# Constants in another order, with padding: other start addresses for w_out_r, the x buffers and the work tiles

## The chip, the cores and the metric

The kernel runs on one core of a Trainium2 chip. The metric is the device time of one execution in microseconds. The core's engines are TensorE (PE; its weight loads are listed as PEld), VectorE (DVE), ScalarE (ACT), GpSimd (POOL) and SyncE (SP, which here only issues DMAs). The on-chip memory has 128 partitions; a tile [P, ...] takes the same bytes in each of them, and where it begins in a partition is its address in what follows.

## The reference

The input x has 8 batches of 3008 tokens with 256 features. Each batch goes through a Fourier layer along the tokens, and the result through a feed-forward layer. Cut to what is computed:

```python
X = np.fft.rfft(x, axis=1)                       # over 3008 tokens
Yr = X.real @ w_r - X.imag @ w_i + b_r
Yi = X.real @ w_i + X.imag @ w_r + b_i
Yr, Yi = soft(Yr), soft(Yi)                      # sign(v) * max(|v| - 0.01, 0)
y = np.fft.irfft(Yr + 1j * Yi, n=3008, axis=1).reshape(24064, 256)
h = y @ w_in                                     # 256 -> 2048
g = np.where(h > 0, h, np.exp(np.minimum(h, 0)) - 1)
out = g @ w_out                                  # 2048 -> 256
```

## The kernel before

The Fourier transforms are done as matrix products in two stages each (3008 = 47 x 64), with twiddle matrices M1 to M4 that the kernel computes at the start. The work of a batch is cut into units: A (first stage, reads x), X (second stage), M (the product with w_r and w_i, and the soft threshold), B and Y (the two stages back). Between A and X and between B and Y the data go through DRAM to change partitions.

The feed-forward layer is the main loop (lines 1050 to 1102). It has 376 steps: 47 blocks of 512 tokens, and in each 8 pairs of 128 hidden features. A step has three parts on TensorE:

- the front (`front_mm`, line 841): four matmuls, two for each of the pair's halves, that multiply w_in_s (bf16, the weights that are loaded) with 512 columns of yT (bf16, the operand that streams). Where a block lies over a batch's end, a matmul is split in two.
- a unit of the Fourier layer of a later batch, put between the front's halves. The planner (`units`, line 945) decides which, by due times and by what is ready. Not every step has one.
- the back (`back`, line 893) of the pair two steps earlier: eight matmuls that load 128 columns of gT (float32r, the activated hidden features) as weights, and stream one row block of w_out_r (float32r, 256 columns, that is 1 KB a partition).

Between front and back of a pair the activation is spread over ScalarE (exp, lines 855 to 858), GpSimd or VectorE (limit, lines 863 and 865) and VectorE (the sum, line 875, which writes gT).

Unit A (line 163) streams x from the buffers xt0 to xt2 in float32r, 512 columns a matmul, with M1 as weights. The other units stream bf16: unit M (line 262) wcat_r, wsum with 256 columns, unit B (line 356) Yt, unit X (line 197) M2, unit Y (line 397) M4.

In time, an opening of about 56 us builds the matrices, brings batch 0 through the Fourier layer and loads the weights (x and w_out_r through GpSimd's DMA queue, line 119 and line 701; all else through SyncE's). Then the main loop runs to the end.

Tiles get their addresses in the order in which they are made. The pool of constants comes first, and each tile takes its size rounded up to 32 bytes, so that a tile moves all that come behind it. The pools of work tiles follow in the order zp, wk1, wk2, wk3, wk4, xtp; then comes the staging pool of the opening, and in its place, after the opening, the pools gatep (the small tile that line 706 writes once), late2 (yT, osb), late3 (Et) and late1 (gT). The lines that set the addresses are 53 to 71 (constants), 425 (x buffers) and 705 (the gate tile):

```python
t = gatep.tile([P, 1], F32, name="gate", tag="gate")
nc.gpsimd.tensor_copy(t[0 : src.shape[0], :], src)
```

Of the kernel before, what the change touches and what calls it, by code (L numbers as in the profile page):

```python
# [8 lines left out]
ALU = mybir.AluOpType  # L9
AF = mybir.ActivationFunctionType  # L10
BF16 = mybir.dt.bfloat16
F32 = mybir.dt.float32
# [3 lines left out]
N1 = 47  # L16
N2 = 64
K1 = 24
# [7 lines left out]
def kernel(  # L26
# [11 lines left out]
    nc = tc.nc  # L38
    P = nc.NUM_PARTITIONS

    B, S, D = x.shape
# [10 lines left out]
    constp = ctx.enter_context(tc.tile_pool(name="constp", bufs=1))  # L52
    M1 = constp.tile([P, P], F32R, name="M1")
    M2 = constp.tile([2 * NR, NS, 2, 2 * K1], BF16, name="M2")
    M3 = constp.tile([P, K1, P], BF16, name="M3")
    M4 = constp.tile([4 * K1, 2 * N1], BF16, name="M4")
    wcat_r = constp.tile([P, 2, 2 * D], BF16, name="wcat_r")
    wsum = constp.tile([P, 2, 2, D], BF16, name="wsum")
    w_in_s = constp.tile([P, 2, DFF], BF16, name="w_in_s")
    w_out_r = constp.tile([P, NFT, E], F32R, name="w_out_r")  # L60
    bias_bc = constp.tile([P, 2 * D], F32, name="bias_bc")
    bias_d = constp.tile([P, D], F32, name="bias_d")
# [2 lines left out]
    dume = constp.tile([P, 1], F32, name="dume")  # L65
    w40 = constp.tile([P, 1], F32, name="w40")
    w41 = constp.tile([P, 1], F32, name="w41")
    arow_t = constp.tile([P, N1], F32, name="arow")
    v4 = constp.tile([P, N1], F32, name="v4")
    r4 = constp.tile([P, N1], F32, name="r4")  # L70
    sg3 = constp.tile([P, K1 // 2], BF16, name="sg3")

    dram = ctx.enter_context(tc.tile_pool(name="dram", bufs=2, space=bass.MemoryType.DRAM))
    zp = ctx.enter_context(tc.tile_pool(name="zp", bufs=1))
# [314 lines left out]
    def unit_Y(b, u, alone=False, on_dve=False):  # L389
# [6 lines left out]
        for j in range(8):  # L396
            nc.tensor.matmul(  # L397
                psv[:, j, 0 : 2 * N1], lhsT=Bs[:, j, dt * P : dt * P + P], rhs=M4[:],
                start=True, stop=True,
# [27 lines left out]
    with tc.tile_pool(name="stagep", bufs=1) as stagep:  # L427
# [19 lines left out]
        dve, pool = nc.vector, nc.gpsimd  # L447

        def iota(name, shape, pattern, base=0, cm=0, dt=F32, out=None):
            t = out if out is not None else stagep.tile(shape, dt, name=name)[:]  # L450
            nc.gpsimd.iota(
                t, pattern=pattern, base=base, channel_multiplier=cm,
                allow_small_or_imprecise_dtypes=True,
            )
            return t

        def row(name, shape):
            return stagep.tile(shape, F32, name=name)
# [45 lines left out]
        arow = iota("arow", [P, N1], [[1, N1]], out=arow_t[:])  # L504
# [37 lines left out]
        def points(g):  # L542

            gs, z = slice(8 * g, 8 * g + 8), slice(0, RZ)
            m_, k_ = mi[z, gs], kv[z, gs]
            dve.tensor_scalar(m_, m_, 63, None, ALU.bitwise_and)
            dve.scalar_tensor_tensor(
                k_, m_, float(N1), kk1[z].unsqueeze(1).to_broadcast([RZ, 8, K1, 2]),
                ALU.mult, ALU.add,
            )  # L550
            if g == 0:
                dve.scalar_tensor_tensor(
                    kv[z, 0, :, 1], mi[z, 0, :, 1], float(N1), kk1[z, :, 0], ALU.mult, ALU.add
                )
            kf = k_.rearrange("p s k t -> p s (k t)")
            dve.tensor_scalar(st[z, gs], kf, S // 2 + 0.5, -0.5, ALU.is_gt, ALU.add)
# [90 lines left out]
        dve.tensor_scalar(m3i[:], m3i[:], 63, None, ALU.bitwise_and)  # L647
        k3 = row("k3", [P, NV])
        dve.scalar_tensor_tensor(k3[:], m3i[:], float(N1), k1t[:], ALU.mult, ALU.add)
        dve.tensor_scalar(sg3[:], k3[:], S // 2 + 0.5, -0.5, ALU.is_gt, ALU.add)  # L650
        points(3)
        phases(3)
        wraps(2)
# [23 lines left out]
    gatep = ctx.enter_context(tc.tile_pool(name="gatep", bufs=2))  # L677
# [24 lines left out]

    def gate(src):

        t = gatep.tile([P, 1], F32, name="gate", tag="gate")
        nc.gpsimd.tensor_copy(t[0 : src.shape[0], :], src)


    def turn_M3(c):
# [6 lines left out]
    def fB(v, on_dve=False):  # L716
        unit_B(0, v, alone=True, on_dve=on_dve)

    load_w_in(0)
    gate(Z_of[0][:, 8, 0:1])  # L720
    for ci in range(3):
        load_x(1, ci)
# [19 lines left out]
    for o, src, sc, bi in ((1, w3, TURN, 0.0), (0, a3, -TURN, hpi[:])):  # L742
        nc.scalar.activation(
            M3f[0][:, :, o * N2 : o * N2 + N2], src[:], AF.Sin, bias=bi, scale=sc
        )
    sgb = sg3[:].unsqueeze(2).to_broadcast([P, K1 // 2, N2])
    nc.vector.scalar_tensor_tensor(
        M3f[1][:, :, 0:N2], M3f[0][:, :, N2:P], 2.0, sgb, ALU.mult, ALU.mult
    )
# [26 lines left out]
    fB(5, True)  # L776
    M4v = M4[:].rearrange("p (a h) -> p a h", h=2)
    for h, w in enumerate((w40, w41)):
# [354 lines left out]
```

## Time and profile before

| what | value |
|---|---|
| median of 3 runs | 884.86 us (883.47 to 884.90) |
| the profiled execution's own time | 882.84 us |
| its span, first to last instruction | 880.8 us |
| mean granted clock of TensorE | 0.998 |
| back matmuls, line 893 | 3008 |
| front matmuls, line 841 | 1728 |
| float32r matmuls on x, line 163 | 96 |
| DMA traffic | 116.55 MB, mean 132 GB/s |

The profile comes from one execution. Its page gives the busy time of each engine, the chain of work that ended last, and groups of instructions with a line number, output and inputs by the program's names, shape, count, total busy time and mean duration of one; behind a second bar stands the idle time of the engine just before them and what ended it. Matmuls overlap, so a listed duration of one is longer than the distance from its start to the next one's. Other views of the same trace give the busy time in chosen stretches, groups with each shape apart, and the instructions in order of time, where neighbours of the same kind are merged: start, time from the first's start to the last's end, engine, line, operation, shape and how many.

### The profile page before, as it was taken

The page shows a single profiled execution, that of the slowest core. Times are in us where ns is not written, and L with a number is a line of the kernel's source. Part 1 is how long each engine was busy: PE and PEld are TensorE (multiplying, and loading weights), DVE is VectorE, ACT ScalarE, POOL GpSimd, SP SyncE. Part 2 cuts the span into 40 slices and gives each one's busy share as a digit, 9 for nine tenths or more (in the row PEclk, how much of TensorE's full clock was granted, in tenths as well). Part 3 has the DMA queues.
Part 4 walks back from the last instruction along what each step waited for, and adds up shares of the span by engine and source line. Part 5 has one row for each costly group of instructions (what it writes and reads, how often), then busy time and mean ns, then how long its engine had stood idle before and what let it go on. Part 6 is the DMA issues. An engine that isn't in the chain of part 4 may idle for free.

```text
span 880.8 us, 18403 instructions
## 1 busy us (share of the span) xinstructions
PE 867.8 (99%) x6745; PEld 672.9 (76%) x6745; DVE 656.7 (75%) x1066; ACT 726.7 (83%) x1217; POOL 651.6 (74%) x981
## 2 busy tenths in 40 slices
PE   8899999999999999999999999999999999999997
PEld 3448777877788777877779777787777877787775
DVE  8767886678767787677876777767776788777775
ACT  6668998899878897899978999789987888786664
POOL 6707995689667887698866888668886699756664
PEclk9999999999999999999999999999999999999999
DMA  8994346743484434643464344553444023431111
GB/s 268 358 264 127 111 113 177 194 148 86 122 251 155 126 114 115 177 140 86 134 189 128 126 131 114 154 167 93 132 122 134 27 65 85 125 81 31 43 30 49
DMA packets 106374, 116.55 MB, mean 132 GB/s; under 512 B 10886, under 2 KB 96012, under 8 KB 103404
## 3 DMA queue, kind: packets, MB, share of 16 engines
q1 hardware_dynamic: 100124, 87.85, 35.9%
q0 software_dynamic: 6016, 27.40, 10.0%
q8 instruction: 53, 0.87, 0.4%
q14 instruction: 37, 0.30, 0.1%
q10 hardware_dynamic: 144, 0.13, 0.0%
HBM read 55.32 MB, written 49.81 MB: 119 GB/s over the span
## 4 chain that ended last, share of the span: by engine, by line
PE 89%; POOL 5%; DVE 3%; DMA 1%; issue 1%; ACT 0%; POOLq 0%; SPq 0%; DVEq 0%
PE ps_o L893 37%; PE hps L841 35%; PE mps L262 5%; PE xps L197 2%; PE yps L397 2%; PE aps L163 2%; POOL Et L863 2%; PE bps L356 1%; PE ips L412 1%; PE mps L214 1%; POOL Y L293 1%; DVE gT L875 1%; PE bps L347 1%; DVE yb L279 1%; DMA xt<-in_x_dram 1%
## 5 line engine op out<-in xcount | busy, mean ns | idle before, releaser
L875 DVE SCALAR_TENSOR_TENSOR gT<-Et,hps 128x512 fp32r<-128x512 f32 x752 | 493.2, 684 | 161.9 <-POOL Et L863 161.2
L893 PE MATMUL ps_o<-w_out_r,gT 128*128 128x256 f32 x3008 | 478.6, 302 | 0.1
L863 POOL TENSOR_SCALAR Et<-Et 128x512 f32<-128x512 f32 x576 | 350.2, 615 | 167.0 <-ACT Et L858 165.6
L893 PEld LDWEIGHTS ps_o<-w_out_r,gT 128*128 128x128 f32 x3008 | 404.7, 189 | 49.7 <-DVE gT L875 0.3
L841 PE MATMUL hps<-yT,w_in_s 128*128 128x512 bf16 (+4 forms) x1728 | 439.6, 355 | 1.1 <-ACT yT L130 0.5
L858 ACT ACTIVATE Et<-hps 128x512 f32<-128x512 f32 x584 | 343.6, 605 | 98.9 <-PE hps L841 95.6
L841 PEld LDWEIGHTS <-w_in_s 128*128 128x128 bf16 x1728 | 121.5, 98 | 55.1 <-issue 16.3
L855 ACT ACTIVATE Et<-hps 128x512 f32<-128x512 f32 x168 | 99.7, 593 | 19.0 <-PE hps L841 18.1
L856 ACT ACTIVATE Et<-Et 128x512 f32<-128x512 f32 x168 | 106.1, 631 | 5.4
L293 POOL TENSOR_TENSOR Y<-yb,clip 128x512 bf16<-128x512 f32 x84 | 108.5, 1292 | 0.3
L288 POOL TENSOR_TENSOR yb<-yb,bias_d 128x256 f32<-128x256 f32 x68 | 49.8, 732 | 30.2 <-DVE yb L279 30.1
L289 POOL TENSOR_SCALAR clip<-yb 128x512 f32<-128x512 f32 x84 | 51.6, 614 | 13.6 <-DVE yb L275 7.4
L246 POOL TENSOR_TENSOR Xd<-XT 128x256 bf16<-128x256 bf16 x84 | 56.5, 672 | 0.0
L130 ACT CAST XT<-xps 128x768 bf16<-128x768 f32 x61 | 48.5, 794 | 2.8 <-PE xps L197 2.8
L130 ACT CAST A<-aps 128x1024 bf16<-128x1024 f32 x45 | 45.3, 1009 | 6.6 <-PE aps L163 6.4
L130 ACT CAST yT<-yps 128x752 bf16<-128x752 f32 x63 | 49.2, 781 | 1.7 <-PE yps L397 1.7
L262 PE MATMUL mps<-wsum,XT 128*128 128x256 bf16 x336 | 50.4, 273 | 0.0
L279 DVE TENSOR_TENSOR yb<-mps,Kb 128x512 f32<-128x512 f32 x68 | 47.0, 692 | 2.5
L278 DVE TENSOR_TENSOR Kb<-mps,bias_bc 128x256 f32<-128x256 f32 x68 | 28.7, 422 | 23.7 <-PE mps L262 23.7
L397 PEld LDWEIGHTS <-Bs 96*128 96x128 bf16 x512 | 28.7, 99 | 15.2 <-DMA Bs<-DB 1.4
L163 PE MATMUL aps<-xt,M 128*128 128x512 f32 x96 | 38.1, 478 | 1.4 <-DMA xt<-in_x_dram 1.0
L197 PEld LDWEIGHTS <-Z 96*128 96x128 bf16 x512 | 28.7, 98 | 13.2 <-issue 2.8
(124 smaller groups left out, 515.4 us busy)
## 6 DMA issues: line engine op xcount, KB each, us to landing
xt<-in_x_dram POOLq DMA_DIRECT2D x21, 1024.0 KB, 5.5
out_dram<-osb SPq DMA_DIRECT2D x158, 128.0 KB
Bs<-DB SPq DMA_DIRECT2D x32, 384.0 KB
DA<-A SPq DMA_DIRECT2D x21, 512.0 KB
DB<-Bz SPq DMA_DIRECT2D x20, 512.0 KB
Z<-DA SPq DMA_DIRECT2D x26, 384.0 KB
Yt<-Y SPq DMA_DIRECT2D x144, 64.0 KB
xt<-in_x_dram POOLq DMA_DIRECT2D x6, 512.0 KB, 5.7
```

Source lines behind the costliest of these rows:

```text
L130: nc.scalar.copy(dst, src)
L246: nc.gpsimd.tensor_tensor(Xd_of[b, k][:], XT[:, :, 0, o : o + P], XT[:, :, 1, o : o + P], ALU.subtract)
L262: nc.tensor.matmul(dst, lhsT=lhs(dt), rhs=rhs(dt), start=dt == 0, stop=dt == 1)
L279: nc.vector.tensor_tensor(two(yb[:]), two(ps[:, 0]), Kb.unsqueeze(1).to_broadcast([P, 2, D]), ALU.add)
L293: nc.gpsimd.tensor_tensor(Y_, two(yb), two(clips[0]), ALU.subtract)
L841: nc.tensor.matmul(hps[s][:, c0:c1], lhsT=w_in_s[:, dt, ft * P : ft * P + P], rhs=yT_of[b][:, dt, t0 : t0 + c1 - c0], start=(dt == 0), sto ...
L855: nc.scalar.activation(e, h, AF.Relu, scale=-1.0)
L856: nc.scalar.activation(e, e, AF.Exp, scale=-1.0)
L858: nc.scalar.activation(e, h, AF.Exp)
L863: nc.gpsimd.tensor_scalar(e, e, 1.0, 0.0, ALU.min, ALU.max)
L875: nc.vector.scalar_tensor_tensor(g_of[self.i][:, p], self.E[:, p], -1.0, self.h[p], ALU.add, ALU.max)
L893: nc.tensor.matmul(po[q][:, i_ % 2, :], lhsT=gT[:, s, i_ * P : i_ * P + P], rhs=w_out_r[:, ft, :], start=(ft == 0 and i_ % 2 == 0), stop=( ...
```

## The change

The constants are made in another order, two of them are wider than what is used of them, and the gate tile has 16 elements in place of 1. M4 goes from before wcat_r to the end; arow and v4 go to before w_out_r; sg3 is made 108 elements wide, of which the first 12 are used as before; the gate copy writes as many elements as its source has, which is one. No instruction is added or taken out, and the order on each engine and queue is as it was. The twiddle matrices M1, M2, M3 keep their addresses.

```diff
     M3 = constp.tile([P, K1, P], BF16, name="M3")
-    M4 = constp.tile([4 * K1, 2 * N1], BF16, name="M4")
     wcat_r = constp.tile([P, 2, 2 * D], BF16, name="wcat_r")
     wsum = constp.tile([P, 2, 2, D], BF16, name="wsum")
     w_in_s = constp.tile([P, 2, DFF], BF16, name="w_in_s")
+    arow_t = constp.tile([P, N1], F32, name="arow")
+    v4 = constp.tile([P, N1], F32, name="v4")
     w_out_r = constp.tile([P, NFT, E], F32R, name="w_out_r")
...
-    arow_t = constp.tile([P, N1], F32, name="arow")
-    v4 = constp.tile([P, N1], F32, name="v4")
     r4 = constp.tile([P, N1], F32, name="r4")
-    sg3 = constp.tile([P, K1 // 2], BF16, name="sg3")
+    sg3 = constp.tile([P, 9 * K1 // 2], BF16, name="sg3")[:, 0 : K1 // 2]
+    M4 = constp.tile([4 * K1, 2 * N1], BF16, name="M4")
...
-        dve.tensor_scalar(sg3[:], k3[:], S // 2 + 0.5, -0.5, ALU.is_gt, ALU.add)
+        dve.tensor_scalar(sg3, k3[:], S // 2 + 0.5, -0.5, ALU.is_gt, ALU.add)
...
-        t = gatep.tile([P, 1], F32, name="gate", tag="gate")
-        nc.gpsimd.tensor_copy(t[0 : src.shape[0], :], src)
+        t = gatep.tile([P, 16], F32, name="gate", tag="gate")
+        nc.gpsimd.tensor_copy(t[0 : src.shape[0], 0 : src.shape[1]], src)
...
-    sgb = sg3[:].unsqueeze(2).to_broadcast([P, K1 // 2, N2])
+    sgb = sg3.unsqueeze(2).to_broadcast([P, K1 // 2, N2])
```

## The prediction

> **What bounds the kernel now.** I read the page's first part and its chain of waits first, then the table of stretches, then the groups of instructions with shapes kept apart, and last the order of time inside one step of the main loop.
>
> From the page, TensorE's line, the chain and its shares:
>
> ```profile
> PE 867.8 (99%) x6745; PEld 672.9 (76%) x6745; DVE 656.7 (75%) x1066; ACT 726.7 (83%) x1217; POOL 651.6 (74%) x981
> ...
> PE 89%; POOL 5%; DVE 3%; DMA 1%; issue 1%; ACT 0%; POOLq 0%; SPq 0%; DVEq 0%
> ```
>
> From the table of stretches (time, then each engine's busy time), one stretch of the main loop:
>
> ```profile
> 62.00:240.00 178.00, 178.00 (x1430) 139.44 (x1428) 137.42 (x220) 159.54 (x264) 137.70 (x197) 1.00 0.49 139
> ```
>
> TensorE is the path: in this stretch it has no idle time at all, its granted clock is 1.00, and no other engine exceeds 90% (ACT, 159.54 of 178.00). So the time of the main loop is the sum of the distances between starts of matmuls. The reader should not take the listed durations for costs (the matmuls overlap), but these distances. They can be worked out from the order of time (start, duration, how many):
>
> ```profile
> 402.48 0.60 PE L841 MATMUL hps<-yT,w_in_s 128*128 128x512 bf16 x2
> 402.73 1.27 PE L893 MATMUL ps_o<-w_out_r,gT 128*128 128x256 f32 x8
> 403.85 0.61 PE L841 MATMUL hps<-yT,w_in_s 128*128 128x512 bf16 x2
> 404.29 0.38 PE L262 MATMUL mps<-wcat_r,Xd 128*128 128x256 bf16 x2
> 404.51 0.60 PE L262 MATMUL mps<-wsum,XT 128*128 128x256 bf16 x4
> 404.95 0.59 PE L841 MATMUL hps<-yT,w_in_s 128*128 128x512 bf16 x2
> ```
>
> The six L262 matmuls (bf16, 256 columns) take 404.95 - 404.29 = 0.66 us: 110 ns each (the trace's start times in ns say 109). The pair of front matmuls at 403.85 takes 0.44 us, of which the trace's starts give 216 ns for an undisturbed one. Between 402.48 and 403.85 lie two of those (0.432) and the eight back matmuls, so these take 0.938 us: 117 ns each, 8 more than bf16 with as many columns. They read w_out_r as float32r, 1 KB a row. Over all steps whose last front matmul is 512 wide, the eight take 925 to 956 ns, 936 in the mean. The 512-wide float32r matmuls of L163, which read xt, stand at 232 to 239 ns in the start times, against 216 for bf16. In the second of an L163 pair no weight load overlaps, and it is as long as the first.
>
> So the only reads of TensorE that cost more than their columns are the float32r moving ones, of w_out_r and xt. The excess of the back matmuls is 3008 x 8 ns = 24 us; of xt's, 96 x 20 ns = 2 us.
>
> **The change part by part.** No instruction is added, removed or moved; no wait and no queue changes; only addresses do. By the program's own allocation in the kernel before, w_out_r lies at byte 41792 of a partition, which is 64 past a multiple of 256 (and 832 past one of 1024); xt0, Z, A, Bz, Yt, Y, yb, clip, Xd, Bs, XT likewise at 64 past a multiple of 256; w_in_s and the wcat/wsum weights too; yT, osb, Et and gT at 128 past one. Adding the tile sizes in the new order, each rounded up to 32 bytes, w_out_r comes to 41984 = 41 x 1024; xt and the work tiles move up by 192 bytes to multiples of 256; wcat_r, wsum and w_in_s go to 128 past one; the gate tile takes 64 bytes instead of 32, twice, which puts yT, osb, Et and gT 256 bytes up, again at 128 past a multiple of 256.
>
> First the parts with one answer, from rows of the same work at two alignments:
>
> ```profile
> L863 POOL TENSOR_SCALAR Et<-Et 128x512 f32<-128x512 f32 x576 | 350.2, 615 | 167.0 <-ACT Et L858 165.6
> L289 POOL TENSOR_SCALAR clip<-yb 128x512 f32<-128x512 f32 x84 | 51.6, 614 | 13.6 <-DVE yb L275 7.4
> L130 ACT CAST XT<-xps 128x768 bf16<-128x768 f32 x61 | 48.5, 794 | 2.8 <-PE xps L197 2.8
> L130 ACT CAST yT<-yps 128x752 bf16<-128x752 f32 x63 | 49.2, 781 | 1.7 <-PE yps L397 1.7
> ```
>
> POOL takes 615 ns on Et (128 past) and 614 on yb and clip (64 past). ACT takes 794 for 768 elements into XT (64 past) and 781 for 752 into yT (128 past): the 13 ns are the 16 elements. So the engines off the path stay as they are: 0 us. And from the groups with shapes kept apart:
>
> ```profile
> L262 PE MATMUL mps<-wsum,XT 128*128 128x256 bf16 x336 | 50.4, 273 | 0.0
> L841 PE MATMUL hps<-yT,w_in_s 128*128 128x256 bf16 x64 | 9.7, 274 | 0.0
> L356 PEld LDWEIGHTS <-M 128*128 128x128 bf16 x144 | 14.1, 98 | 9.3
> L262 PEld LDWEIGHTS <-XT 128*128 128x128 bf16 x336 | 32.9, 98 | 3.8
> ```
>
> A bf16 moving row costs 273 ns at 64 past (wsum) and 274 at 0 or 128 past (yT); a bf16 weight load 98 from M3 (128 past) and 98 from XT (64 past). So all bf16 reads: 0 us. The float32r weight loads (gT, M1) stay at 128 past: 0 us. The gate copy is one element a partition as before, once, in the opening: 0.
>
> The DMAs: in the opening three transfers stand in the chain, x for 5.88 us, the DB store 2.79, Bs 3.88. The page's landing times for x are 5.5 and 5.7 us for two sizes; I take that spread, 0.2 us, as what an address could do either way, so three times 0.2 gives bounds of -0.6 and +0.6 and I take 0. In the main loop TensorE covers them. [...]
>
> The one term left is the float32r moving reads, for which no row has another alignment. Its ends: none of the excess goes (the bf16 rows, 0 us), or all (the 109 ns of bf16: 8 x 109 = 872 against 936 ns, 64 ns x 376 steps = -24 us). Between them lies a row of the same matmul itself: the distances of back matmuls in the trace are not one value, but a low one of 113 to 114 ns and a high one of 117 to 119, in patterns that recur from step to step, whichever row of w_out_r is read. So 117 is no limit of the port or of the weight load, and the stall is in the reading of the row. I take it that a row which begins on a boundary is read in the low way throughout: 117.0 to 113.4, 3.6 ns x 3008 = -10.8 us. Of that, TensorE's 89% of the chain counts, and in the rest POOL, DVE and issue are late next (POOL's L293 and L863 stand there in the chain): -9.6 us. xt, in proportion, 72 matmuls of the main loop x 9 ns: -0.6 us. Sum: -10.2 us. The profiled execution took 882.84 us (span 880.8 and 2.0 around it): 872.6. The median of the runs shown, 884.86, is 2.0 above that execution: 874.7, say 875.
>
> **The rivals.** *Nothing changes.* The excess is a matter of 4 bytes a column and not of where a row starts. For it: bf16 rows of the same 1 KB (front matmuls, 512 columns) cost the same at every start. Against: 113 and 117 occur for the same addresses, so the byte rate alone does not set it. Time 883 to 886, 884.9. [...]
>
> *Slower: the steps lock into the high pattern.* Place: the eight back matmuls. The moving rows and the gT weights are read at the same time; their distance goes from -192 to -128 bytes modulo 1024, and which pattern a step falls into is a matter of such phases. If all steps took the commoner high value, 945 instead of 936 ns, it is 9 x 376 = +3.4 us; at the highest, 956, +7.5. It decides once over half of the steps that are now under 936 go over. Time 888 to 892, in the middle 890. Against: the low pattern is there now with the rows off the boundary.
>
> *The whole excess goes.* Back matmuls at bf16's 109 ns: -24 us less a tenth, 863. For it: xt's excess is about twice w_out_r's high one, as for a cost by the KB. Against: the lowest distance seen is 113.
>
> **How the numbers follow.** Forecast (low pattern, 869 to 881 us by how many steps take it): 0.36. Nothing: 0.32. Slower: 0.23. The whole excess: 0.09. About 0.2%, 1.8 us, is what a measurement of this kernel can tell from no change. Faster is 0.36 + 0.09 = 0.45, same 0.32, slower 0.23. The range goes from 867, which leaves out the whole excess and little else, to 891, the better part of the slower case.
>
> **What would show it.** Right: the eight back matmuls between two fronts take 0.91 us instead of 0.94, the L163 pair less than 0.47, and everything else as before: POOL 615, ACT 781, bf16 distances 109 and 216, the same chain with TensorE's share the same or a little lower. Wrong: back steps of 0.94 with the same two values (nothing), or of 0.95 (slower); or a gain in the opening's DMAs alone. What would make it wrong is that the low distance is a matter of the phase between weight loads and rows and not of the rows' start.

## The result: slower by 0.6%

The changed kernel takes 888.72 us (median, 887.88 to 888.85) against 884.35 for the kernel before in the runs beside it. The ratio is 1.0058 with a 95% interval of 1.0047 to 1.0068. The forecast of 875 us had the sign wrong; the time is that of the rival in which the steps lock into the high pattern (888 to 892 us). Whether its cause is the right one, the experiments have to show.

The profiled execution took 888.65 us, its span is 886.8, 6.0 us above that of before. The page of the changed kernel, TensorE's line and the chain's shares:

```profile
PE 872.4 (98%) x6745; PEld 676.7 (76%) x6745; DVE 657.2 (74%) x1066; ACT 727.7 (82%) x1217; POOL 653.1 (74%) x981
...
PE 92%; DVE 3%; POOL 2%; DMA 2%; issue 1%; ACT 1%; POOLq 0%; DVEq 0%; SPq 0%
```

TensorE was the path and is it more than before (92% of the chain, 89% before). The table of stretches of the changed kernel shows that it is still without a gap, at the same clock, and gets less done in the same 178 us, 1426 matmuls for 1430 (the main loop begins about 1 us later in this profile, so the two stretches do not hold quite the same work):

```profile
62.00:240.00 178.00, 178.00 (x1426) 139.42 (x1424) 136.83 (x219) 159.04 (x264) 136.33 (x194) 1.00 0.49 138
```

Where the time went is seen in the groups with shapes kept apart. Of the changed kernel:

```profile
L893 PE MATMUL ps_o<-w_out_r,gT 128*128 128x256 f32 x3008 | 483.7, 303 | 0.1
L262 PE MATMUL mps<-wsum,XT 128*128 128x256 bf16 x336 | 50.4, 273 | 0.0
L163 PE MATMUL aps<-xt,M 128*128 128x512 f32 x96 | 38.1, 478 | 2.5 <-DMA xt<-in_x_dram 2.1 <-DVE A L366 0.3 <-ACT a L587 0.2
```

And of the kernel before:

```profile
L893 PE MATMUL ps_o<-w_out_r,gT 128*128 128x256 f32 x3008 | 478.6, 302 | 0.1
L163 PE MATMUL aps<-xt,M 128*128 128x512 f32 x96 | 38.1, 478 | 1.4 <-DMA xt<-in_x_dram 1.0 <-DVE A L366 0.3
```

The back matmuls are busy 5.1 us longer. The matmuls on xt are at 38.1 us in both, although xt moved too, and the bf16 ones at 50.4 in both. The order of time of the changed kernel, over the same kinds of step as the one shown of before:

```profile
405.75 0.61 PE L841 MATMUL hps<-yT,w_in_s 128*128 128x512 bf16 x2
406.01 1.30 PE L893 MATMUL ps_o<-w_out_r,gT 128*128 128x256 f32 x8
407.15 0.61 PE L841 MATMUL hps<-yT,w_in_s 128*128 128x512 bf16 x2
407.59 0.38 PE L262 MATMUL mps<-wcat_r,Xd 128*128 128x256 bf16 x2
407.81 0.60 PE L262 MATMUL mps<-wsum,XT 128*128 128x256 bf16 x4
408.25 0.59 PE L841 MATMUL hps<-yT,w_in_s 128*128 128x512 bf16 x2
```

From 405.75 to 407.15 it is 1.40 us, where the step before had 1.37; the six bf16 matmuls still take 0.66. Over all steps whose last front matmul is 512 wide, the eight back matmuls take 950.1 ns in the mean, 936.1 before; the times from start to start make the difference. Before, 128 of 318 steps were below 937 ns; now there is none, and the lowest is 944. 14 ns x 376 steps = 5.3 us.

The view by source line gives the first and the last start of a back matmul, that is the length of the main loop without the opening (minimum, median and maximum duration; then the two times in us). Before, and after the change:

```profile
L893 PE MATMUL ps_o<-w_out_r,gT x3008: 276/281/476, 61.7 to 875.3; 128*128 128x256 f32 x188
```

```profile
L893 PE MATMUL ps_o<-w_out_r,gT x3008: 274/281/471, 62.9 to 881.3; 128*128 128x256 f32 x188
```

That is 813.6 and 818.4 us, 4.8 more. The other 1.2 us of the spans' difference lie in the opening, whose end varies from one profile to the next (by the same view, the first back matmul starts at 61.7 to 63.3 us in the kernels below that are as fast as before), so no price of the change is read from it.

### The profile page after: what moved, and what is told of

Its sections match the earlier page's. It is cut to its first block, busy times and chain, and to the rows that moved or that the text cites. A ratio compares the mean times of both kernels' runs of the same rounds, so it can differ in the third digit from the quotient of the medians.

```text
span 886.8 us, 18403 instructions
## 1 busy us (share of the span) xinstructions
PE 872.4 (98%) x6745; PEld 676.7 (76%) x6745; DVE 657.2 (74%) x1066; ACT 727.7 (82%) x1217; POOL 653.1 (74%) x981
## 4 chain that ended last, share of the span: by engine, by line
PE 92%; DVE 3%; POOL 2%; DMA 2%; issue 1%; ACT 1%; POOLq 0%; DVEq 0%; SPq 0%
PE ps_o L893 39%; PE hps L841 37%; PE mps L262 6%; PE xps L197 2%; PE yps L397 2%; PE aps L163 2%; PE bps L356 2%; PE mps L214 1%; PE bps L347 1%; DMA xt<-in_x_dram 1%; DVE gT L875 1%; POOL Et L863 1%; DMA Bs<-DB 0%; DVE yb L279 0%; DMA DB<-A 0%
## 5 line engine op out<-in xcount | busy, mean ns | idle before, releaser
L893 PE MATMUL ps_o<-w_out_r,gT 128*128 128x256 f32 x3008 | 483.7, 303 | 0.1
L262 PE MATMUL mps<-wsum,XT 128*128 128x256 bf16 x336 | 50.4, 273 | 0.0
L163 PE MATMUL aps<-xt,M 128*128 128x512 f32 x96 | 38.1, 478 | 2.5 <-DMA xt<-in_x_dram 2.1
```

The costliest lines, as they stand in the source:

```text
L163: nc.tensor.matmul(ps[:, j, :], lhsT=M1[:], rhs=xt[:, 4 * uu + 2 * j : 4 * uu + 2 * j + 2, :], start=True, stop=True,)
L262: nc.tensor.matmul(dst, lhsT=lhs(dt), rhs=rhs(dt), start=dt == 0, stop=dt == 1)
L893: nc.tensor.matmul(po[q][:, i_ % 2, :], lhsT=gT[:, s, i_ * P : i_ * P + P], rhs=w_out_r[:, ft, :], start=(ft == 0 and i_ % 2 == 0), stop=( ...
```

## The experiments

What had to be told apart: **P**, the place at which a row of w_out_r starts; **D**, the distance between the first byte of the weights (gT) and that of the row, modulo some power of two; **G**, the place of gT or of the other work tiles. (A distance in bytes is always this one, between addresses; the prediction's distances in ns are times from one start to the next.) "Step" is the mean time of the eight back matmuls, worked out from the start times as in the prediction; some traces lack about a hundred records of front matmuls, and the steps beside a missing one are left out (288 to 318 steps remain). "Main" is last minus first start of a back matmul.

### Only the rows moved

```diff
-    arow_t = constp.tile([P, N1], F32, name="arow")     # was behind w_out_r
+    arow_t = constp.tile([P, N1], F32, name="arow")     # made right before w_out_r
```

> Only w_out_r moves, to a multiple of 1024 as in the changed kernel (arow is made before it); all other tiles are where they were. Mean of the eight back matmuls of a step: 936 ns before, 950 after the change. Theory P (where a row of w_out_r starts sets it): 950 ns, 888.5 us. Theory G (the place of gT or of the other work tiles sets it): 936 ns, 884.4 us. Theory D (the distance of gT's place from the row's, modulo 1024, sets it): the distance is -384, which neither kernel has, so a value of its own between 925 and 956 ns, 880 to 891 us.

Measured: 887.44 us, ratio 1.0039 (1.0026 to 1.0052); step 948.9 ns; main 817.6 us. Moving w_out_r alone brings 13 of the 14 ns. That is against G, and it leaves P and D.

### All but the rows

```diff
 # in the changed kernel
-    v4 = constp.tile([P, N1], F32, name="v4")           # was before w_out_r
+    v4 = constp.tile([P, N1], F32, name="v4")           # made before r4
```

> The changed kernel with w_out_r back at its old place (v4 is made behind it), everything else as changed. Theory P: 936 ns, 884.4 us. Theory G: 950 ns, 888.7 us. Theory D: the distance is +64, a value of its own.

Measured: 884.06 us, ratio 1.0002 (0.9991 to 1.0012); step 940.5 ns; main 813.9 us. With the rows back, x buffers and work tiles on multiples of 256 bytes cost nothing and bring nothing. P expects that; D allows it. The distance here is +64; the step is some 4 ns above that of before, which these runs' times do not show.

### The rows and gT moved together

```diff
 # in the kernel with only the rows moved
-        return late1.tile([P, n_], dt, name=name, tag=f"gT{k % 3}")[:]
+        lead = 48 if k % 3 == 2 else 0
+        return late1.tile([P, lead + n_], dt, name=name, tag=f"gT{k % 3}")[:, lead:]
```

> As the run with only the rows moved, and the gT buffers moved up by the same 192 bytes, so that their distance is that of before. Theory D: 936 ns, 884.4 us as before. Theory P: 950 ns, 888.5 us. Theory G: gT starts at a place that neither kernel has, a value of its own.

Measured: 882.90 us, ratio 0.9996 (0.9984 to 1.0007); step 935.1 ns; main 814.3 us. The rows begin on multiples of 1 KB as in the changed kernel, and the loss is gone. This is D's number, and P is out.

### A table in one run

```diff
-    w_out_r = constp.tile([P, NFT, E], F32R, name="w_out_r")
+    w_out_t = constp.tile([P, NFT // 2, 2 * E + 16], F32R, name="w_out_r")
+    w_out_p = w_out_t[:, :, 0 : 2 * E]
...
+        lead = {2: 0, 0: 16, 1: 48}[k % 3]
+        return late1.tile([P, lead + n_], dt, name=name, tag=f"gT{k % 3}")[:, lead:]
```

(M4 and the gate tile are as in the kernel before; arow, v4 and r4 go into a buffer that is free in the opening, which makes the room, and sg3 is widened by what is left, so that all other tiles stay in place.)

> Each pair of rows of w_out_r begins 64 bytes further on than the pair before (modulo 1024: 832, 896, 960, 0, 64, 128, 192, 256), and the three gT buffers begin at 640, 704 and 896; everything else is in place, so one run gives the back step for 24 combinations. Two more loads of w_out_r in the opening. Theory P: the step depends on the pair alone, 936 ns for the first, 950 for the fourth, alike in all three buffers. Theory D: it depends on the distance alone, so that the first buffer with pair k, the second with pair k+1 and the third with pair k+4 agree: 936 ns at -192, 950 at -128. Theory G: on the buffer alone.

Measured: 885.27 us in its one run. The mean step in ns, by pair of rows (where it starts modulo 1024) and gT buffer (likewise), with the distance modulo 256 in brackets:

| pair at | gT at 640 | gT at 704 | gT at 896 |
|---|---|---|---|
| 832 | 933 (64) | 947 (128) | 931 (64) |
| 896 | 951 (0) | 932 (64) | 951 (0) |
| 960 | 945 (192) | 953 (0) | 937 (192) |
| 0 | 954 (128) | 944 (192) | 948 (128) |
| 64 | 928 (64) | 947 (128) | 936 (64) |
| 128 | 952 (0) | 930 (64) | 952 (0) |
| 192 | 941 (192) | 954 (0) | 933 (192) |
| 256 | 952 (128) | 944 (192) | 950 (128) |

Each entry is the mean of 6 to 16 steps. No row and no column of the table has one value. The distances sort it: 928 to 936 at 64 and 947 to 954 at 0 and 128; 192 lies between, and spreads over 933 to 945. So D holds against P and G, and its period is 256 bytes, not 1024: the entries at 64 have distances that differ by 256 and 512. The kernel before stands at 64 (640 - 832 = -192), the changed one at 128 (896 - 0 = 896 = 3 x 256 + 128).

### The gate tile narrow again

The period gives a sharper test. In the changed kernel, the wider gate tile is what keeps gT at 128 past a multiple of 256 behind tiles that are moved up to multiples of it.

```diff
 # in the changed kernel
-        t = gatep.tile([P, 16], F32, name="gate", tag="gate")
+        t = gatep.tile([P, 1], F32, name="gate", tag="gate")
```

> The changed kernel with the gate tile as narrow as before: w_out_r, x buffers and work tiles begin where the change puts them, but yT, osb, Et and gT lie 64 bytes lower, at 64 past a multiple of 256. The distance of gT from the rows becomes 64 modulo 256, that of before. Theory D: 936 ns a step, 884.2 us, the whole loss gone with rows still on multiples of 1 KB. Theory P: 950 ns, 888 us.

Measured: 883.96 us, ratio 1.0006 (0.9997 to 1.0016); step 936.4 ns; main 813.8 us. Undoing the padding of a tile that is written once, in the opening, undoes the loss, with w_out_r, the x buffers and the work tiles where the change puts them. The group of back matmuls of this kernel:

```profile
L893 PE MATMUL ps_o<-w_out_r,gT 128*128 128x256 f32 x3008 | 478.7, 302 | 0.1
```

It is 483.7 in the changed kernel and 478.6 before.

### gT alone moved, in the kernel before

```diff
 # in the kernel before
+        lead = 16 if k % 3 == 2 else 0
+        return late1.tile([P, lead + n_], dt, name=name, tag=f"gT{k % 3}")[:, lead:]
```

> The kernel before with the gT buffers alone moved up by 64 bytes; w_out_r and all else stay. The distance becomes 128 modulo 256, that of the changed kernel. Theory D: 950 ns a step, 888.5 us. Theory P: 936 ns, 884.2 us, since no row of w_out_r is moved.

Measured: 888.92 us, ratio 1.0057 (1.0037 to 1.0077); step 951.5 ns; main 819.5 us. The same loss without touching w_out_r. Its back matmuls, whose line number is one higher for the inserted line:

```profile
L894 PE MATMUL ps_o<-w_out_r,gT 128*128 128x256 f32 x3008 | 484.1, 303 | 0.1
```

### No tile moved, the loads read elsewhere

What remained was whether the meeting of the two reads counts, or where the gT tiles lie for the engines that write them.

```diff
 # in the changed kernel
-                    po[q][:, i_ % 2, :], lhsT=gT[:, s, i_ * P : i_ * P + P],
+                    po[q][:, i_ % 2, :], lhsT=gT[:, s, min(i_ * P + 48, 304) : min(i_ * P + 48, 304) + P],
```

> The changed kernel, no tile moved; only the weight loads of the back matmuls read gT from 192 bytes further on (columns 48, 176, 304 and 304 in place of 0, 128, 256 and 384), so the products are of shifted columns of gT and the last 128 are computed from columns that were used before. The distance of the load's first byte from the row's becomes 64 modulo 256. Theory D, told as a meeting of two reads of TensorE: 936 ns a step, 884.2 us. If it is the place of the gT tile itself that counts (by VectorE's writes to it, say): 950 ns, 888.5 us.

Measured: 883.84 us, ratio 0.9999 (0.9988 to 1.0010); step 938.4 ns; main 814.0 us. Every tile lies as in the changed kernel and is written as there; only the loads start 192 bytes further on, and the loss is gone. Its back matmuls:

```profile
L893 PE MATMUL ps_o<-w_out_r,gT 128*128 128x256 f32 x3008 | 478.8, 302 | 0.1
```

So it is TensorE's two reads, of weights and of the row that streams, and the distance between their first bytes: 938.4 ns a step at 64, 950.1 at 128. That the weights are those of the next matmul is a reading of the trace, where the next load starts 2 to 5 ns behind a back matmul's start (189 behind the first of a step); by distance the two cannot be told apart, since the blocks of gT lie 512 bytes from one another.

A distance of 64 does not make every step fast. In the six whole kernels that have it (before, all but the rows, rows and gT, narrow gate, loads read elsewhere, and the last one below), 33 to 50% of the steps take less than 937 ns, and the means are 935.1 to 940.5. In the three at 128 (changed, rows only, gT only) not one step does, and the means are 948.9 to 951.5.

### Finer tables, and the search for a better place

```diff
-    w_out_t = constp.tile([P, NFT // 2, 2 * E + 16], F32R, name="w_out_r")
+    w_out_t = constp.tile([P, NFT // 2, 2 * E + 4], F32R, name="w_out_r")
...
-        lead = {2: 0, 0: 16, 1: 48}[k % 3]
+        lead = {2: 0, 0: 32, 1: 48}[k % 3]
```

> As the table before, in steps of 16 bytes: the pairs of rows begin at 832, 848, ... 944 modulo 1024, the three gT buffers at 640, 768 and 960, so the distance (gT minus row) takes every multiple of 16 modulo 256. Theory D, sharpened by the first table (about 931 ns at 64, 942 at 192, 950 to 952 at 0 and 128, all modulo 256): these four come again, in whichever buffer and pair they fall, and the steps between show whether the good places are a few bytes wide (some below 931) or 64 wide. Theory P: the step follows the pair and not the distance.

Measured: 888.47 us in its one run. The mean step by distance modulo 256:

| distance | 0 | 16 | 32 | 48 | 64 | 80 | 96 | 112 | 128 | 144 | 160 | 176 | 192 | 208 | 224 | 240 |
|---|---|---|---|---|---|---|---|---|---|---|---|---|---|---|---|---|
| ns | 952 | 943 | 949 | 953 | 935 | 955 | 952 | 951 | 952 | 951 | 950 | 953 | 947 | 950 | 940 | 941 |

Twelve of the sixteen distances cost 947 to 955 ns. 64 is the best and its neighbours 48 and 80 are among the worst. At 192 this run has 947 where the first table had 933 to 945, with 8 steps alone to tell it by.

The next table takes steps of 4 bytes.

```diff
-    w_out_t = constp.tile([P, NFT // 2, 2 * E + 4], F32R, name="w_out_r")
+    w_out_t = constp.tile([P, NFT // 2, 2 * E + 1], F32R, name="w_out_r")
...
-        lead = {2: 0, 0: 32, 1: 48}[k % 3]
+        lead = {2: 0, 0: 7, 1: 36}[k % 3]
```

> The table in steps of 4 bytes around the two good places: pairs of rows at 832, 836, ... 860, gT buffers at 640, 668 and 816, so the distance modulo 256 runs from 36 to 92 and from 212 to 240. Theory D with a good place that is exactly 64: about 932 ns at 64 alone, 945 to 955 at its neighbours of 4 and 8 bytes. If the good place is some 16 bytes wide: 930 to 940 from about 56 to 72. A distance that is better than 64 by over 5 ns would be a place for a faster kernel.

Measured: 891.39 us in its one run, the slowest. No distance is below 940 ns here; the two combinations at distance 64 stand at 941 (before's very places, where the first table had 933) and 947 (row at 860, gT at 668, both 12 past a multiple of 16). So a step may also feel the steps beside it, and 64 alone is not enough here. What sorts this table is not the distance but the row's start within 16 bytes:

| the row starts, past a multiple of 16 | steps, ns by the six combinations |
|---|---|
| 0 | 941, 946, 946, 950, 952, 952 |
| 4 bytes | 958, 966, 966, 968, 969, 970 |
| 8 bytes | 960, 961, 962, 962, 964, 967 |
| 12 bytes | 941, 942, 943, 947, 947, 949 |

So P has a part of its own, but inside 16 bytes, where the kernels before and after do not differ.

Last, another place with distance 64, at which the first table had 928 ns:

```diff
 # in the kernel before: arow, lam_n and hpi made right before w_out_r
+    arow_t = constp.tile([P, N1], F32, name="arow")
+    lam_n = constp.tile([P, 1], F32, name="lam_n")
+    hpi = constp.tile([P, 1], F32, name="hpi")
     w_out_r = constp.tile([P, NFT, E], F32R, name="w_out_r")
```

> The kernel before with w_out_r alone 256 bytes up (arow, lam_n and hpi are made before it): the distance is -448, again 64 modulo 256. Theory D with a period of 256: 936 ns and 884.2 us as before, or, if the 928 ns that the first table has at this distance hold for a whole kernel, 8 x 376 less, 881 us, faster by 0.3%. A theory in which the place modulo 1024 counts has no reason for either and allows 950 ns, 888 us.

Measured: 883.22 us, ratio 0.9996 (0.9985 to 1.0006); step 936.1 ns; main 813.6 us. The period of 256 holds for a whole kernel; the 928 ns of the table did not. No layout that was run beats the kernel before beyond its interval: it stood at the best of the distances tried.

## Why the prediction was wrong

**Right.** The path: TensorE's stream of matmuls, with the back matmuls of w_out_r as the only term that the change moves. The rows of the terms put at nothing stand as before: POOL's limit is at 617 ns (615), ACT's casts at 794 and 781, the bf16 times from start to start at 109 and 216. The kernel with the narrow gate has the change's places of w_out_r, the x buffers and the work tiles, and its DMAs, and takes as long as before (ratio 1.0006), so the loads of the opening cost nothing that shows.

**Wrong, the step that failed:** "I take it that a row which begins on a boundary is read in the low way throughout." The low and the high distances were read rightly as two ways in which the same matmul runs, but they were ascribed to the row's start. Rows on multiples of 1 KB gave 948.9 ns (rows alone), 935.1 (with gT moved too), 936.4 (narrow gate) and 938.4 (loads 192 bytes on). In its place stands the distance between weights and row modulo 256, which the change turned from 64 to 128. The sum looked at each read by itself ("The float32r weight loads (gT, M1) stay at 128 past: 0 us") and so had no term for the pair. The term that was forecast at -9.6 us came out at +4.8 (main loop) to +5.3 (14 ns x 376).

**The xt term** (-0.6 us) was wrong with it: the second of an L163 pair stands at 238 ns before and after. One reading was off too: between starts, the first of a pair is not as long as the second but takes 420 ns in the median; the second's load begins only 189 ns behind the first's start.

These matmuls also limit what was found. M1 begins at 128 past a multiple of 256, and xt moved from 64 past to 0 (by the padding of sg3, the only constant that is made wider than its use). So their distance went from 64 to 128, as that of gT and w_out_r did. Yet their group takes 38.1 us in both kernels, and in the first of a pair, beside which a float32r load runs, the time from that load's start to the next matmul's is 231 ns in the median in both; a gain of 4 ns, that from the high time of a back matmul to the low one, would show there. A distance of 64 is thus no gain for every float32r matmul; it is shown for the back matmuls alone, and why not for these stays open.

**The slower rival** named the place, the cause (the distance between the two reads) and a price of +3.4 to +7.5 us, and got 0.23. What was said against it, that the low pattern is there with the rows off the boundary, was no argument: it showed only that the row's start is not needed for it. That the steps' sequences recurred whichever row was read could have pointed to the second read. The modulus was guessed at 1024 and is 256, and the steps do not all take the commoner high value of 945 ns: they run from 944 to 961, with a mean of 950.

**Nothing changes** (0.32) took the excess for a matter of 4 bytes a column and not of where a row starts. The bytes are the same in both kernels, and the mean steps differ by 14 ns (936.1 and 950.1), so they do not decide it alone. Both layouts start rows on multiples of 16 bytes (41792 and 41984). Off those, the table in steps of 4 bytes does show a part for the start: 4 or 8 bytes past a multiple cost some 15 to 18 ns a step in the mean, 12 bytes nothing.

**What stays open** is the mechanism below the distance. Were it the load beside it that costs the row's reading time, the fast distances would be the ones without loss. But the second matmul of an L163 pair has no load beside it until the last 4 or 5 ns before the next start. In the kernel before, weight loads (PEld) and matmuls around such a pair:

```profile
401.79 0.41 PEld L163 LDWEIGHTS aps<-xt,M 128*128 128x128 f32 x2
401.82 0.82 PE L163 MATMUL aps<-xt,M 128*128 128x512 f32 x2
402.48 0.11 PEld L841 LDWEIGHTS <-w_in_s 128*128 128x128 bf16 x2 [0.28 <-issue]
```

It takes 238 ns for 512 columns, 119 for 256, and eight times 119 is 952: the step at an ordinary distance. This suggests that what is special is not the loss at 128 but the gain at 64, though the comparison is between matmuls of two shapes. Why a load at that distance should make the row's reading faster than no load at all was not found.

## What to carry to other kernels

In this kernel the distance between the places of float32r weights and rows, modulo 256 bytes, was worth 1.5% of the back matmuls (14 of 936 ns), and one small tile ahead of gT changed it (the gate tile: 936.4 ns with 1 element, 950.1 with 16). The matmuls on x, at 38.1 us with either distance, show that it need not be so elsewhere. After a change of the layout, where TensorE is the path, compare the times between starts of each group of its matmuls before anything else. Aligning each tensor by itself says nothing of the pair: with rows on multiples of 1 KB the step took 948.9 ns in one kernel and 935.1 in another. A table of distances comes out of one run, by giving rows and buffers of the same loop different starts; its best entry (928 ns here) has to be tried in a whole kernel (936).

## What was not expected of the hardware

- The cost of these float32r matmuls depends on where the weights lie: eight take 935 to 941 ns in whole kernels at a distance of 64 modulo 256 and 949 to 952 at 128; in the tables most other distances cost 947 to 955, the neighbours at 16 bytes on either side of 64 among them.
- The float32r matmuls on x, with the same two distances, cost the same at both (38.1 us for 96).
- bf16 matmuls show nothing of this: before and after the change those of unit M take 109 ns, with distances of 0 and 128, and undisturbed front matmuls 216 ns, with 64 and 192 before and 0 and 128 after.
- A float32r row that starts 4 or 8 bytes past a multiple of 16 costs 958 to 970 ns for eight, one that starts 0 or 12 past 941 to 952.
- Padding a tile that is written once before the main loop moved the whole kernel by 0.5% (883.96 us with the gate tile narrow, 888.72 wide).
